# Rewriting the opening of an attention-and-MLP kernel: two blocks by halves of 256 tokens, one explicit order of operations, wider weight casts

## The chip, the cores and the metric

The kernel runs on one core of one Trainium2 chip. The metric is device time in microseconds (us). It was 305.51 us before the change (median of 3 runs, 305.02 to 306.14).

The names of the engines in the profile are PE (TensorE), PEld (TensorE's weight loads), ACT (ScalarE), DVE (VectorE), POOL (GpSimd) and SP (SyncE, which only issues DMAs here). "PEclk" is the share of TensorE's full clock that was granted. It stands at 1.00 also where the trace has no record of the clock; a slow clock there shows only in the pace of the products.

## The reference

q, k and v have the shape 8 x 8 x 576 x 64. Attention is computed within chunks of 64 tokens. Its output x has 4608 rows of 512, and it feeds an MLP with a gate that depends on the channel:

```python
# cut from the reference
scores = scale * np.matmul(q_c, k_c.transpose(0, 1, 2, 4, 3))   # chunks of 64 tokens
attn = np.exp(scores - np.max(scores, axis=-1, keepdims=True))
attn = attn / (np.sum(attn, axis=-1, keepdims=True) + 1e-09)
x = np.matmul(attn, v_c)            # then reordered to [4608, 512]
h = x @ w_in                        # 512 -> 2048
g = h * (1.0 / (1.0 + np.exp(-beta * h)))
return (g @ w_out).astype(np.float32)   # 2048 -> 512
```

Everything arrives and leaves in float32. The kernel multiplies in bfloat16, so every input is loaded and then cast.

## The kernel before

The work is cut into nine blocks of 512 tokens. For each block the kernel loads q, k and v, casts them, transposes q and k, and computes scores, exp, `attend` (the product with v), `normalize` and `turn` (the transpose of x). Then come `mm1` (the product with w_in, tanh on ScalarE, g on VectorE) and `mm2` (the product with w_out). In the first blocks all of this has to wait for data: 8 MB of weights, and 3 MB of q, k and v for each block.

A small helper class records operations per engine in program order and derives the semaphores from what each one reads and writes (`K(...)` names a piece of memory). So the order in which the Python code calls the functions is the order in which each in-order engine and DMA queue works. In this kernel that order comes from events `at(time, function, ...)`, which are sorted by their time:

```python
at(-100, make_constants)
at(-100, load_beta)

at(-99, load_qk, 0, 0)
at(-99, load_qk, 0, 1)
at(-98, load_v, 0)
for j in range(4):
    at(-97, load_w_in, j)
    at((-43, 1.5, 5.5, 9.5)[j], cast_w_in, j, ("pool",) * 4)
    at((-42.8, 1.7, 5.7, 9.7)[j], load_w_out, j)
    at((15, 20, 24, 25)[j], cast_w_out, j, ("pool",) * 4)
at(-43.5, load_qk, 1, 0)
at(-43.5, load_qk, 1, 1)
at(-42.9, load_v, 1, (0,))
at(-42.7, load_v, 1, (1,))
at(10, load_qk, 2, 0)
at(10, load_qk, 2, 1)
at(10, load_v, 2)

# ... (blocks 1 and 2)
    t0, u = base(blk - 1) + 2, 1
    loads = 24.5 if blk == 3 else t0 - 22
    for which in range(2):
        at(loads, load_qk, blk, which)
    at(loads + 0.1, load_v, blk)
    for i in range(4):
        at(35.5 if blk == 3 else t0 - 15.9, cast_qk, blk, i // 2, i % 2, "pool")
# ... (attention of the later blocks)
for blk in range(NB):
    for n in range(16):
        at(base(blk) + n, mm1, blk, n, (n + 2) % 4 if blk < 1 else n % 2)
# ...
events.sort(key=lambda e: (e[0], e[1]))
for _, _, fn, args in events:
    fn(*args)
```

The weights are loaded in quarters of 1 MB and cast by GpSimd in four instructions of 512 columns. beta is loaded near the front, on ScalarE's DMA queue:

```python
def load_beta():
    def f(e):
        with nc.allow_non_contiguous_dma(reason="beta is tiny"):
            return e.dma_start(beta_raw[:, :], beta.rearrange("(t p) -> p t", p=128))
    P.dma("act", f, writes=[K("beta_raw")])
    P.op("dve", lambda e: e.tensor_single_scalar(
        beta_half[:, :], beta_raw[:, :], 0.5, ALU.mult),
        reads=[K("beta_raw")], writes=[K("beta_half")])
# ...
def load_v(blk, us=(0, 1)):
    s, h = blk % NVS, slice(4 * us[0], 4 * us[-1] + 4)
    for b, c, m, at in chunk_pairs(blk):
        def f(e, b=b, c=c, at=at, m=m):
            r = 64 * (at % 2)
            return e.dma_start(vstage[r:r + 64 * m, s, at // 2, h, :],
                               v[b][h, 64 * c:64 * (c + m), :].rearrange("h t d -> t h d"))
        P.dma("sp", f, writes=[K("vstage", s, u, at + i, v=blk)
                               for u in us for i in range(m)])

def load_w_in(j):
    s = j % NWS

    def f(e):
        a = w_in[:, 512 * j:512 * (j + 1)].rearrange("(c p) f -> p c f", p=128)
        return e.dma_start(wstage[:, s, :].rearrange("p (c f) -> p c f", c=4), a)
    P.dma("sp", f, writes=[K("wstage", s, v=j)])

def load_w_out(j):
    s = (4 + j) % NWS

    def f(e):
        a = w_out[512 * j:512 * (j + 1), :].rearrange("(t p) d -> p t d", p=128)
        return e.dma_start(wstage[:, s, :].rearrange("p (t d) -> p t d", t=4), a)
    P.dma("sp", f, writes=[K("wstage", s, v=4 + j)])
# ... (cast_w_in likewise)
def cast_w_out(j, engines):
    s = (4 + j) % NWS
    for i, eng in enumerate(engines):
        dst = w_out_bf[:, 4 * j + i, :]
        src = wstage[:, s, 512 * i:512 * (i + 1)]
        if eng == "act":
            P.op("act", lambda e, d=dst, a=src: e.activation(d, a, AF.Copy),
                 reads=[K("wstage", s, v=4 + j)], writes=[K("w_out", 4 * j + i)])
        else:
            P.op(eng, lambda e, d=dst, a=src: e.tensor_copy(d, a),
                 reads=[K("wstage", s, v=4 + j)], writes=[K("w_out", 4 * j + i)])

```

The product with w_in always takes all 512 tokens of a block, writes one bank of the PSUM tensor F, and needs the whole x of its block:

```python
def mm1(blk, t, bank):
    sx, sg, T = blk % NXT, blk % 2, NT * blk + t
    for c in range(NC):
        P.op("pe", lambda e, c=c: e.matmul(
            F[:, bank, :], w_in_bf[:, c, 128 * t:128 * t + 128], x_of(sx, c),
            start=(c == 0), stop=(c == NC - 1)),
            reads=[K("w_in", t // 4, c), K("xT", sx, c // 2, v=blk)],
            writes=[K("F", bank, v=("h", T))])
    P.op("act", lambda e: e.activation(tt[:, T % 3, :], F[:, bank, :], AF.Tanh,
                                       scale=beta_half[:, t:t + 1]),
         reads=[K("F", bank, v=("h", T)), K("beta_half")], writes=[K("tt", T % 3, v=T)])
    P.op("dve", lambda e: e.scalar_tensor_tensor(
        g2[:, sg, t, :], tt[:, T % 3, :], 1.0, F[:, bank, :], ALU.add, ALU.mult),
        reads=[K("F", bank, v=("h", T)), K("tt", T % 3, v=T)], writes=[K("g", sg, t, v=blk)])
```

The softmax here doesn't subtract the row's maximum and nothing guards it: scores larger than these inputs give would overflow.

## Time and profile before

The median of three runs is 305.51 us. The profiled run took 303.35 us, with a span of 301.5 us and no loss of clock on record, so it is at the fast end of this kernel's runs.

The first view gives the busy time of each engine in five stretches of the profiled run of the kernel before. The columns are the stretch and its length, then the busy time and the count of instructions for PE, PEld, DVE, ACT and POOL, then PEclk, the share of the DMA engines' time, and GB/s.

```profile
...
core 0: us, PE busy (x) PEld busy (x) DVE busy (x) ACT busy (x) POOL busy (x), PEclk, DMA share, GB/s
0.00:20.00 20.00, 8.42 (x174) 6.56 (x175) 6.94 (x10) 8.62 (x11) 5.34 (x16) 1.00 1.02 269
20.00:36.00 16.00, 15.54 (x93) 7.63 (x92) 10.82 (x16) 10.78 (x16) 12.61 (x21) 1.00 1.04 325
36.00:50.00 14.00, 11.54 (x181) 5.81 (x179) 7.01 (x10) 7.65 (x12) 8.38 (x18) 1.00 1.08 349
50.00:84.00 34.00, 31.61 (x329) 15.56 (x330) 20.15 (x25) 17.97 (x27) 19.24 (x21) 1.00 1.05 271
84.00:290.00 206.00, 205.94 (x1640) 94.00 (x1639) 93.67 (x136) 103.84 (x163) 71.80 (x62) 1.00 0.64 148
...
```

TensorE does nothing else than work from 84 us on: 205.94 us of 206. A gain can only come from the first 84 us. There it idles for 11.6 us in the first 20 us, and for 0.5, 2.5 and 2.4 us in the next three stretches. DMA is full over these stretches: its share is about 1 on average in each of the first four.

The second view is the timeline of the kernel before, cut to three starts: the last cast of v for block 0, the four casts of the first w_in quarter, and the first product with w_in. Columns: start, duration, engine, source line, operation, output and input, count; in brackets the idle time just before and what ended it.

```profile
...
15.29 0.62 POOL L314 CAST v_bf<-vstage 128x512 bf16<-128x512 f32 x1 [0.52 <-DMA vstage<-in_v_dram]
...
18.01 2.29 POOL L294 CAST w_in_bf<-wstage 128x512 bf16<-128x512 f32 x4 [2.10 <-DMA wstage<-in_moe_w_in_dram]
...
20.28 1.06 PE L441 MATMUL F<-xT,w_in_bf 128*128 128x512 bf16 x2
...
```

The first product starts at 20.28 us, 2.3 us after the first quarter of w_in has landed.

The third view lists what TensorE waited for in the opening of the kernel before, from 20 to 84 us. Columns: the waiting engine and line, the releaser, total us, number of waits, the longest.

```profile
...
PE F L441 <- DVE g L449: 0.9, 2, 0.6
PE A L389 <- POOL v_bf L314: 0.8, 1, 0.8
PE F L389 <- ACT E L374: 0.8, 2, 0.6
PE A L423 <- DVE x_sb L405: 0.8, 1, 0.8
PE A L367 <- DVE qkO L314: 0.8, 1, 0.8
PE A L341 <- POOL qkcast L314: 0.4, 1, 0.4
PE F L423 <- DVE x_sb L405: 0.3, 1, 0.3
```

These waits are small, spread out, and of different kinds: v casts on GpSimd, copies and normalizing on VectorE, exp on ScalarE. They add up to 4.8 us. Measured another way, the time from the first product to the last (278.1 us) less all its products at their warm pace (269.0 us: 53.7 for the opening, 215.3 after it) is 9.1 us. That counts also the slow clock at the start (a product every 0.43 us until 22.60 us, and every 0.216 us after) and the fractions of a microsecond that a list of waits leaves out.

The fourth view is the chain of waits that ended last in the kernel before, cut to its weight loads (start, length, what):

```profile
...
31.85 6.37 DMA wstage<-in_moe_w_out_dram
38.67 11.18 DMA wstage<-in_moe_w_out_dram
49.91 1.53 POOL w_out_bf L306 x3
...
```

In this stretch the chain goes through the loads of w_out, for 17.6 us.

The page's list of the costliest groups of the kernel before gives the cost of tanh (L446) and g (L449) per product of 512 tokens. After the shapes come the count, the busy time in all and the mean ns of one, then the idle time before them and its releasers.

```profile
...
L449 DVE SCALAR_TENSOR_TENSOR g<-tt,F 128x512 bf16<-128x512 bf16 x144 | 98.9, 688 | 129.5 <-ACT tt L446 129.3
L446 ACT ACTIVATE tt<-F,beta_half 128x512 bf16<-128x512 f32 x144 | 98.9, 687 | 113.2 <-PE F L441 111.3
...
```

Both take 0.69 us against 0.863 us of TensorE for the same product. There is little room in those two engines while products of w_in follow one another.

### The profile page before, as it was taken

The numbers are of one execution on the slowest core, as the hardware profiler recorded it, in microseconds if no ns is written. First come the engines' busy times: TensorE is split into PE (matmuls) and PEld (weight loads), VectorE is DVE, ScalarE is ACT, GpSimd is POOL, SyncE is SP. The second block draws the span as 40 slices with busy tenths as digits, with TensorE's granted clock in tenths as the row PEclk, the third lists the DMA queues.
The fourth block names the chain that finished last, engine by engine and source line by source line (L and its number), as shares of the span: only waits on it lengthen the run. The fifth ranks groups of instructions, "written<-read, shape, count | busy, mean of one in ns | idle before, by whom it ended". The sixth has DMA issues, their size and how long they took to land.

```text
span 301.5 us, 5783 instructions
## 1 busy us (share of the span) xinstructions
PE 281.4 (93%) x2448; PEld 133.2 (44%) x2448; DVE 138.6 (46%) x194; ACT 150.6 (50%) x230; POOL 117.4 (39%) x134
## 2 busy tenths in 40 slices
PE   1579979988999999999999999999999999999995
PEld 1444543544444444444444444444444444444442
DVE  1447853446755543553364336433643373343300
ACT  2537754664555446544644464446444644554411
POOL 1258677742780962098085408640660000000000
PEclk9999999999999999999999999999999999999999
DMA  7999999999999579979926992798471122000121
GB/s 192 269 386 362 272 335 364 243 328 213 255 290 193 143 238 216 185 187 315 223 73 187 306 206 72 215 295 160 66 90 39 48 71 72 35 35 35 57 85 70
DMA packets 106161, 55.96 MB, mean 186 GB/s; under 512 B 79000, under 2 KB 97432, under 8 KB 106136
## 3 DMA queue, kind: packets, MB, share of 16 engines
q1 hardware_dynamic: 98944, 46.15, 63.9%
q10 hardware_dynamic: 7192, 9.45, 9.5%
q8 instruction: 19, 0.31, 0.4%
q14 instruction: 6, 0.05, 0.0%
HBM read 36.71 MB, written 9.44 MB: 153 GB/s over the span
## 4 chain that ended last, share of the span: by engine, by line
PE 80%; DMA 7%; DVE 4%; ACT 3%; SPq 1%; POOL 1%; issue 1%; ACTq 1%
PE F L456 38%; PE F L441 37%; DMA wstage<-in_moe_w_out_dram 6%; PE A L367 2%; PE A L389 2%; DMA qkstage<-in_k_dram 2%; SPq L256 1%; DVE qkO L314 1%; DVE x_sb L405 1%; ACT tt L446 1%; DVE g L449 1%; POOL w_out_bf L306 1%; ACT ostage L461 1%; ACT qkO L312 1%; ACTq L469 1%
## 5 line engine op out<-in xcount | busy, mean ns | idle before, releaser
L449 DVE SCALAR_TENSOR_TENSOR g<-tt,F 128x512 bf16<-128x512 bf16 x144 | 98.9, 688 | 129.5 <-ACT tt L446 129.3
L446 ACT ACTIVATE tt<-F,beta_half 128x512 bf16<-128x512 f32 x144 | 98.9, 687 | 113.2 <-PE F L441 111.3
L441 PE MATMUL F<-xT,w_in_bf 128*128 128x512 bf16 x576 | 147.0, 381 | 1.0 <-DVE g L449 0.9
L456 PE MATMUL F<-w_out_bf,g 128*128 128x512 bf16 x576 | 145.1, 379 | 0.0
L456 PEld LDWEIGHTS F<-w_out_bf,g 128*128 128x128 bf16 x576 | 55.5, 98 | 65.0
L441 PEld LDWEIGHTS F<-xT,w_in_bf 128*128 128x128 bf16 x576 | 54.2, 98 | 65.5 <-DVE g L449 2.4
L314 POOL COPY qkO<-qkT 128x1024 bf16<-128x1024 bf16 x22 | 42.8, 1988 | 59.2 <-DMA qkT<-qkcast 47.8
L314 POOL CAST qkcast<-qkstage 128x1024 bf16<-128x1024 f32 x32 | 32.9, 1043 | 22.8 <-DMA qkstage<-in_q_dram 11.1
L461 ACT ACTIVATE ostage<-F 128x512 f32<-128x512 f32 x36 | 21.5, 598 | 18.7 <-PE F L456 18.6
L314 POOL CAST v_bf<-vstage 128x512 bf16<-128x512 f32 (+1 forms) x40 | 23.3, 619 | 13.4 <-DMA vstage<-in_v_dram 13.4
L374 ACT ACTIVATE E<-A 128x512 bf16<-128x512 f32 x36 | 20.5, 593 | 1.3 <-PE A L367 1.3
L405 DVE TENSOR_TENSOR x_sb<-A,rec 128x1024 bf16<-128x1024 f32 x16 | 19.6, 1224 | 0.6
L341 PE MATMUL F<-identity,qkcast 128*128 128x128 bf16 x32 | 4.1, 311 | 8.6 <-DVE qkcast L314 6.9
L306 POOL CAST w_out_bf<-wstage 128x512 bf16<-128x512 f32 x16 | 9.2, 618 | 5.6 <-DMA wstage<-in_moe_w_out_dram 5.6
L294 POOL CAST w_in_bf<-wstage 128x512 bf16<-128x512 f32 x16 | 9.2, 617 | 4.3 <-DMA wstage<-in_moe_w_in_dram 3.8
L367 PEld LDWEIGHTS A<-qkO 64*64 64x64 bf16 x576 | 6.4, 113 | 8.7 <-issue 6.5
L367 PE MATMUL A<-qkO 64*64 64x64 bf16 x576 | 8.2, 200 | 2.0 <-ACT qkO L312 1.2
L389 PE MATMUL A<-v_bf,E 64*64 64x65 bf16 x512 | 8.2, 198 | 1.3 <-POOL v_bf L314 0.8
L389 PEld LDWEIGHTS A<-v_bf,E 64*64 64x64 bf16 x512 | 5.9, 109 | 7.9 <-issue 5.5
L341 PEld LDWEIGHTS F<-identity,qkcast 128*128 128x128 bf16 x32 | 3.1, 141 | 9.4 <-DVE qkcast L314 7.2
L312 ACT ACTIVATE xT<-F 128x1024 bf16<-128x1024 bf16 x3 | 3.1, 1024 | 5.4 <-PE F L423 5.4
L341 PE MATMUL A<-identity,qkcast 128*128 128x128 bf16 x64 | 4.9, 219 | 0.5 <-POOL qkcast L314 0.4
(31 smaller groups left out, 48.3 us busy)
## 6 DMA issues: line engine op xcount, KB each, us to landing
out_dram<-ostage ACTq DMA_DIRECT2D x36, 256.0 KB, 3.4
qkstage<-in_q_dram SPq DMA_DIRECT2D x32, 256.0 KB, 4.7
qkstage<-in_k_dram SPq DMA_DIRECT2D x32, 256.0 KB, 5.8
vstage<-in_v_dram SPq DMA_DIRECT2D x28, 256.0 KB, 6.5
wstage<-in_moe_w_in_dram SPq DMA_DIRECT2D x4, 1024.0 KB, 10.0
wstage<-in_moe_w_out_dram SPq DMA_DIRECT2D x4, 1024.0 KB, 8.3
vstage<-in_v_dram SPq DMA_DIRECT2D x16, 128.0 KB, 4.7
qkstage<-in_q_dram SPq DMA_DIRECT2D x8, 128.0 KB, 3.3
```

The costliest lines, as they stand in the source:

```text
L306: P.op(eng, lambda e, d=dst, a=src: e.tensor_copy(d, a), reads=[K("wstage", s, v=4 + j)], writes=[K("w_out", 4 * j + i)])
L314: P.op(eng, lambda e: e.tensor_copy(dst, src), reads, writes)
L341: P.op("pe", lambda e, n=n, i=i: e.transpose(dst[:, i, n, :], qkcast[:, which, 2 * half + n, i, :, :].rearrange("p h d -> p (h d)"), ident ...
L367: return e.matmul(A[64 * g:64 * g + 64, 2 * u + hb, col:col + 64], kT[r, 2 * cc + g, :], qT[r, 2 * cc + g, :])
L374: P.op("act", lambda e: e.activation(E[:, bank, :], A[:, bank, :], AF.Exp, scale=0.125), reads=[K("A", bank, v=("s", blk))], writes=[K("E" ...
L389: return e.matmul(ps[64 * half:64 * half + 64, bank, col:col + 65], E[r, 2 * u + hb, 256 * w + 64 * cc:256 * w + 64 * cc + 64], v_bf[r, sa ...
L405: P.op("dve", lambda e: e.tensor_tensor(x_sb[:, u, :, :, :].rearrange("p g c (h d) -> p (g c h) d", h=2).rearrange("p (b t) d -> p b t d", ...
L441: P.op("pe", lambda e, c=c: e.matmul(F[:, bank, :], w_in_bf[:, c, 128 * t:128 * t + 128], x_of(sx, c), start=(c == 0), stop=(c == NC - 1)) ...
L446: P.op("act", lambda e: e.activation(tt[:, T % 3, :], F[:, bank, :], AF.Tanh, scale=beta_half[:, t:t + 1]), reads=[K("F", bank, v=("h", T) ...
L449: P.op("dve", lambda e: e.scalar_tensor_tensor(g2[:, sg, t, :], tt[:, T % 3, :], 1.0, F[:, bank, :], ALU.add, ALU.mult), reads=[K("F", ban ...
L456: P.op("pe", lambda e, t=t: e.matmul(F[:, bank, :], g2[:, sg, t, 128 * s:128 * s + 128], w_out_bf[:, t, :], start=(t == 0), stop=(t == NT ...
L461: P.op("act", lambda e: e.activation(ostage[:, N % NOS, :], F[:, bank, :], AF.Copy, scale=0.5), reads=[K("F", bank, v=("o", N))], writes=[ ...
```

## The change

The idea is to let TensorE start on half a block. Blocks 0 and 1 are handled in halves of 256 tokens from the loads to the first product, so that half of the products can start when half of x is made. Products may use banks of both PSUM tensors, A and F. w_in comes in five pieces instead of four (the first two are half as wide), and each weight piece is cast by one GpSimd instruction. The times and formulas for everything up to time 78 are replaced by one written list of 390 operations. From block 3 or 4 on the order is the old one. "No dummy products" is part of the description of the change; neither kernel has any.

```diff
-        tt = sb("tt", [128, 3, 512], BF16)
+        NTT = 4
+        tt = sb("tt", [128, NTT, 512], BF16)
-        NOS = 3
+        NOS = 4
...
+        W_IN = ((0, 256), (256, 256), (512, 512), (1024, 512), (1536, 512))
...
+        def cast_w_in(j):
+            f0, n = W_IN[j]
+            src, keys = stage_in(j)
+            P.op("pool", lambda e: e.tensor_copy(w_in_bf[:, :, f0:f0 + n], src),
+                 reads=keys, writes=[K("w_in", t) for t in range(f0 // 128, (f0 + n) // 128)])
...
-        def mm1(blk, t, bank):
+        def mm1(blk, t, bank, ps=F, psname="F", halves=(0, 1)):
+            r = slice(256 * halves[0], 256 * halves[-1] + 256)
             for c in range(NC):
                 P.op("pe", lambda e, c=c: e.matmul(
-                    F[:, bank, :], w_in_bf[:, c, 128 * t:128 * t + 128], x_of(sx, c),
+                    ps[:, bank, r], w_in_bf[:, c, 128 * t:128 * t + 128], x_of(sx, c, halves),
...    (load_qk, load_v, scores, exp_half, attend, normalize, turn_pe: halves or pairs likewise)
-        at(-101, load_act_table)
-        at(-100, make_constants)
-        at(-100, load_beta)
-        at(-99, load_qk, 0, 0)
...    (all other events before time 78)
+        first = [
+            (load_qk, 0, 0, (1,)), (cast_qk, 0, 0, 1, "act"), (load_qk, 0, 1, (0,)),
+            (load_qk, 0, 0, (0,)), (load_qk, 0, 1, (1,)), (load_v, 0, (1,)), (load_v, 0, (3,)),
+            (load_v, 0, (0,)), (load_v, 0, (2,)), (load_w_in, 3), (cast_qk, 0, 1, 0, "act"),
+            (load_qk, 1, 1, (0,)), (load_act_table,), (make_constants,), (cast_qk, 0, 0, 0, "dve"),
...
+            (transpose_pe, 0, 1, 1, F, "F", 1, "dve"), (load_w_in, 2), (scores, 0, 0, (0,)),
+            (scores, 0, 3, (0,)), (load_beta,), (scores, 0, 2, (0,)), (exp_half, 0, 1, 0),
...    (390 operations in all)
+        events = [(-1, i, fn, args) for i, (fn, *args) in enumerate(first)] + [
+            e for e in events if e[0] >= START]
```

## The prediction

> **What bounds it now.** The timeline of TensorE and the chain of waits show four stages of the 301.5 us span.
> (1) Head: the first product starts at 20.28 us. The last k load lands at 10.51; then cast (1.06), transpose (1.05), copy (1.03), scores, exp, attend, normalize (1.23), turn and copy follow one another. The first w_in quarter lands at 18.01 only, its first cast ends at 18.6.
> (2) Opening, 20.28 to 83.09: I count 136 and 72 big products, 96 transposes and 288 small attention products. At the warm spacing in the trace (4 big products in 0.863, 8 transposes in 0.45, 32 small ones in 0.38) this is 53.7 us of 62.8, so about 9 us are lost: about 1.2 on a cold clock (0.43 per product until 22.6), the rest in eleven gaps of 0.3 to 1.0 (attend behind v casts and exp, scores behind copies, products behind VectorE). DMA is busy throughout; the last w_out quarter lands at 49.9.
> (3) 83.09 to 298.4: TensorE alone, no gap.
> (4) 3.1 us of eviction and store.
>
> **What the change can reach.** Only (1) and (2). From about block 3 the order is the old one; the fourth tt and ostage buffers buy nothing there.
>
> Head: the same 4 MB (q, k, v, then 1 MB of w_in) must land before any product, so w_in arrives at about 18.0 as before, and is now cast as one piece: from the GpSimd casts of 512 and 1024 columns (0.617, 1.043) I estimate 1.9 for 2048, ready at 19.9. The halved attention should have x for the first half at about 19.6. First product about 20.0, a gain of 0.3 only. It still starts cold: the Trainium skill, "TensorE: Matmul & The Clock Gate", Part 1, has half rate until about 3.4 us of sustained activity; before's trace agrees (0.43 falling to 0.216 at 22.6, after work that began at 18.03). I expect 1.3 lost.
>
> Opening: x of block 1 is made by halves, half of block 1's products no longer wait for all of v, w_out is loaded between the block-1 pieces, seven or eight PSUM banks (A as well as F) take products, v casts are spread. By my count of bytes (2.7 us per MB, 4.7 for v) w_out quarters are cast at about 36, 41, 46 and 50, each just ahead of its use, so DMA should not stall TensorE. Most gaps should go.
>
> Added cost: products of 256 columns cost TensorE nothing (128-column transposes already run at 0.056 each), but 64 tanh and 64 g half-pieces cost ScalarE and VectorE about 0.47 and 0.42 by estimate, against 0.69 per whole: some 8 and 5 us more. VectorE, with 1.22 copies between, is as full as TensorE in block 0; the banks hide most of it. I expect 1 to 2 us of waits there and 1 later, so 3.5 lost in place of 9.
>
> **Prediction.** Gain 0.3 + 5.5, less some slippage: about 5.5 us. Time 300.0 us, range 296.8 to 303.5; faster by over 2%: 0.38, within 2%: 0.60, slower: 0.02.
>
> **What would show it.** First product at 19.5 to 20.5, spacing cold (0.21 per 256 columns) till about 23; TensorE near gapless from 24 to 80, with waits on VectorE's g of 1 to 2 us in 20 to 38; last w_out landing at 47 to 51; the steady stage and tail unchanged; the total gained entirely before 84 us.
>
> **What would make it wrong.** Better: w_in lands earlier, or gaps vanish altogether (298 or below). Worse: VectorE or ScalarE bound on half pieces; in-order queues, where one late load or cast stalls everything behind it in the fixed order; late w_out; the clock going cold again; wide GpSimd casts slower than estimated.

## The result, and the profile after

A ratio in this document is the mean time of one kernel's fast runs over that of the other's fast runs of the same rounds, so it is not quite the ratio of the medians beside it. The brackets are 95% intervals.

| | before | after |
|---|---|---|
| median of 4 runs | 305.26 us (304.50 to 306.14) | 301.10 us (300.85 to 301.71) |
| ratio | | 0.9866 [0.9834, 0.9898] |
| profiled run, span | 303.35, 301.5 us | 301.26, 299.5 us |
| first product | 20.28 us | 21.54 us |
| last product ends | 298.35 us | 296.35 us |

The new kernel is faster by 1.3%, which is "the same" at the 2% line. Neither profiled run has a loss of clock on record after its slow start. Their spans differ by 2.0 us only, since the profiled run of before was faster than its timed runs. What follows explains these 2.0 us from the traces. A repeat on another chip gave a ratio of 0.9933 [0.9899, 0.9967] (below), which is also about 2.0 us. Why the first measurement shows twice that is not settled. It lies with the kernel before: its median was 305.26 us here and 303.87 in the repeat, that of the changed kernel 301.10 and 301.40.

The same five stretches, kernel after, with the same columns:

```profile
...
0.00:20.00 20.00, 7.71 (x169) 6.01 (x170) 6.29 (x13) 8.32 (x12) 3.66 (x12) 1.00 0.96 237
20.00:36.00 16.00, 14.73 (x137) 12.28 (x136) 12.61 (x29) 13.56 (x30) 10.27 (x8) 1.00 1.07 365
36.00:50.00 14.00, 12.73 (x207) 8.05 (x206) 10.77 (x22) 7.75 (x17) 6.04 (x6) 1.00 1.06 280
50.00:84.00 34.00, 33.56 (x370) 22.04 (x369) 22.32 (x43) 22.68 (x45) 12.85 (x13) 1.00 1.07 278
84.00:290.00 206.00, 205.95 (x1675) 94.41 (x1673) 97.32 (x140) 105.10 (x166) 71.66 (x60) 1.00 0.65 152
...
```

The steady stage is unchanged (205.95 us of 206), so the whole difference arises before 84 us. In the first 20 us TensorE does 0.71 us less than before, and in the next 16 us 0.81 us less. From 36 to 50 it does 1.19 us more, and from 50 to 84 it does 1.95 us more and idles for 0.44 us only. The change loses in the head and wins in the opening.

The head, from the timeline of the kernel after: the halving of beta on VectorE, the last GpSimd cast of v, the first cast of w_in, and the first product.

```profile
...
16.87 0.17 DVE L243 TENSOR_SCALAR beta_half<-beta_raw 128x16 f32<-128x16 f32 x1 [2.43 <-DMA beta_raw<-in_moe_beta_dram]
...
16.96 0.62 POOL L316 CAST v_bf<-vstage 128x512 bf16<-128x512 f32 x1 [1.51 <-DMA vstage<-in_v_dram]
...
19.50 1.90 POOL L295 CAST w_in_bf<-wstage 128x2048 bf16<-128x2048 f32 x1 [1.92 <-DMA wstage<-in_moe_w_in_dram]
...
21.54 0.80 PE L464 MATMUL F<-xT,w_in_bf 128*128 128x256 bf16 x3
...
```

The last cast of v starts 1.67 us later than before, at 16.96 us. The first piece of w_in is cast from 19.50 us instead of 18.01. VectorE waits 2.43 us for beta. The first product comes 1.26 us later than before, where the prediction had it 0.3 us earlier. The same 4 MB have to arrive first in both kernels, so something slowed them. The following two fences show the DMA queues from 12 to 16 us, before and then after. The first line has packets, bytes and throughput. The others have, for each queue, packets, MB, and the time their packets took as a share of 16 engines. Packets in flight overlap, so the shares may add up to more than 100%.

```profile
...
DMA packets 2088, 1.12 MB, mean 281 GB/s; under 512 B 1754, under 2 KB 1754, under 8 KB 2088
...
q1 hardware_dynamic: 2088, 1.12, 121.7%
...
```

```profile
...
DMA packets 4232, 0.67 MB, mean 166 GB/s; under 512 B 4169, under 2 KB 4169, under 8 KB 4232
...
q1 hardware_dynamic: 2168, 0.66, 94.9%
q10 hardware_dynamic: 2064, 0.01, 35.8%
...
```

In the kernel after, 2064 packets with 0.01 MB in all run on ScalarE's queue (q10). They are the load of beta: 2048 numbers of four bytes, each in a packet of its own. These packets take 35.8% of the 16 engines for 4 us, which is 11 ns of one engine for each (0.358 x 16 x 4 us / 2064), or 1.4 us of all 16, and throughput drops from 281 to 166 GB/s. In the kernel before the same load ran between 1 and 5 us, when the main queue had little to do: it carried 0.58 MB in the first 5 us. The Trainium skill, "DMA: Bandwidth & Descriptors", states that each DMA engine takes turns between the queues that have work, packet by packet (Queues, rings and completion order). The drop of the main queue, from 121.7% to 94.9%, agrees with that. So a queue of tiny packets can take a large share of the engines' time from a queue of larger ones.

What TensorE waited for in the opening of the kernel after, in the same form as before, from 21.5 to 90 us:

```profile
...
PE A L464 <- POOL w_in_bf L295: 0.9, 2, 0.6
PE F L482 <- POOL w_out_bf L305: 0.8, 1, 0.8
PE F L403 <- POOL v_bf L316: 0.5, 2, 0.3
PE A L403 <- POOL v_bf L316: 0.3, 1, 0.3
PE A L343 <- POOL qkcast L316: 0.2, 1, 0.2
```

The waits of the kernel before on VectorE and ScalarE are gone. Those that are left, 2.7 us, are on GpSimd's casts of what DMA brought. From first to last product, less 269.0 us at the warm pace, the loss is now 5.8 us (before: 9.1).

The chain of waits of the kernel after goes through w_out as before (a load and the cast behind it). In front of that, from the start to 26.58 us, it is SyncE's issuing of loads almost alone, where in the kernel before it runs through the computing engines from 10.59 to 31.85 us. Whether the issuing itself is slow, or only waits for the full DMA engines, no run tested; with beta first, issuing the four v loads took 4.92 us in place of 5.61, so it is at least in part a wait:

```profile
...
34.03 9.59 DMA wstage<-in_moe_w_out_dram
43.68 1.91 POOL w_out_bf L305
...
```

The four w_out casts start at 37.80, 43.68, 48.94 and 53.87 us (before: 38.27, 43.33, 47.13, 49.91). The list asks for them later on purpose, behind pieces of block 1.

The groups of the kernel after between 20 and 60 us, kept apart by form, give the cost of the half-size pieces of tanh (L469) and g (L473):

```profile
...
L469 ACT ACTIVATE tt<-A,beta_half 128x256 bf16<-128x256 f32 x27 | 12.4, 474 | 4.7 <-PE A L464 4.7
L473 DVE SCALAR_TENSOR_TENSOR g<-tt,A 128x256 bf16<-128x256 bf16 x27 | 11.2, 419 | 4.0 <-ACT tt L469 3.7
...
```

A half takes 0.474 and 0.419 us, so two halves cost 0.26 us more on ScalarE and 0.15 us more on VectorE than one whole (0.69). This was predicted to the second digit. No wait on g of the predicted 1 to 2 us is on the list, though; the extra banks may hide it, which was not tested.

### The profile page after: what moved, and what is told of

The parts are those of the page before. It is cut to its first block, busy times and chain, and to the rows that moved or that the text cites. A ratio compares the mean times of both kernels' runs of the same rounds, so it can differ in the third digit from the quotient of the medians.

```text
span 299.5 us, 6088 instructions
## 1 busy us (share of the span) xinstructions
PE 281.0 (94%) x2576; PEld 145.5 (49%) x2576; DVE 149.3 (50%) x244; ACT 158.7 (53%) x268; POOL 104.5 (35%) x95
## 4 chain that ended last, share of the span: by engine, by line
PE 79%; SPq 9%; DMA 8%; POOL 1%; ACT 1%; DVE 1%; issue 1%; ACTq 0%
PE F L482 39%; PE F L464 34%; SPq L260 5%; DMA wstage<-in_moe_w_out_dram 3%; DMA qkstage<-in_q_dram 2%; PE A L464 2%; DMA vstage<-in_v_dram 2%; SPq L289 2%; PE A L403 2%; SPq L271 2%; PE A L371 2%; POOL w_out_bf L305 1%; DVE qkO L316 0%; ACTq L496 0%; ACT ostage L488 0%
## 5 line engine op out<-in xcount | busy, mean ns | idle before, releaser
L473 DVE SCALAR_TENSOR_TENSOR g<-tt,F 128x512 bf16<-128x512 bf16 (+1 forms) x140 | 88.5, 634 | 108.1 <-ACT tt L469 107.8
L469 ACT ACTIVATE tt<-F,beta_half 128x512 bf16<-128x512 f32 (+1 forms) x140 | 89.9, 645 | 96.4 <-PE F L464 92.8
L464 PE MATMUL F<-xT,w_in_bf 128*128 128x512 bf16 (+1 forms) x560 | 130.3, 359 | 0.2
L488 ACT ACTIVATE ostage<-F 128x512 f32<-128x512 f32 x36 | 21.5, 598 | 19.7 <-PE F L482 19.7
L426 DVE TENSOR_TENSOR x_sb<-A,rec 128x1024 bf16<-128x1024 f32 (+1 forms) x19 | 20.6, 1084 | 0.7
L464 PE MATMUL A<-xT,w_in_bf 128*128 128x256 bf16 x144 | 19.9, 275 | 0.9 <-POOL w_in_bf L295 0.9
L469 ACT ACTIVATE tt<-A,beta_half 128x256 bf16<-128x256 f32 x36 | 16.4, 474 | 6.3 <-PE A L464 6.3
L316 POOL CAST v_bf<-vstage 128x512 bf16<-128x512 f32 x28 | 16.5, 625 | 6.5 <-DMA vstage<-in_v_dram 6.5
L473 DVE SCALAR_TENSOR_TENSOR g<-tt,A 128x256 bf16<-128x256 bf16 x36 | 14.7, 418 | 4.9 <-ACT tt L469 4.6
L464 PEld LDWEIGHTS A<-xT,w_in_bf 128*128 128x128 bf16 x144 | 13.9, 99 | 4.4 <-DVE g L473 1.5
L295 POOL CAST w_in_bf<-wstage 128x2048 bf16<-128x2048 f32 (+1 forms) x5 | 7.8, 1555 | 7.2 <-DMA wstage<-in_moe_w_in_dram 5.9
```

The source lines that it names most:

```text
L316: P.op(eng, lambda e: e.tensor_copy(dst, src), reads, writes)
L426: P.op("dve", lambda e: e.tensor_tensor(dst, o[:, :, :, 0:64], r.unsqueeze(3).to_broadcast([128, nb, 4, 64]), ALU.mult), reads=src + [K("r ...
L464: P.op("pe", lambda e, c=c: e.matmul(ps[:, bank, r], w_in_bf[:, c, 128 * t:128 * t + 128], x_of(sx, c, halves), start=(c == 0), stop=(c == ...
L469: P.op("act", lambda e: e.activation(tt[:, T % NTT, r], ps[:, bank, r], AF.Tanh, scale=beta_half[:, t:t + 1]), reads=[K(psname, bank, v=(" ...
L473: P.op("dve", lambda e: e.scalar_tensor_tensor(g2[:, sg, t, r], tt[:, T % NTT, r], 1.0, ps[:, bank, r], ALU.add, ALU.mult), reads=[K(psnam ...
L488: P.op("act", lambda e: e.activation(ostage[:, N % NOS, :], ps[:, bank, :], AF.Copy, scale=0.5), reads=[K(psname, bank, v=("o", N))], writ ...
```

## The experiments

The table gives all twelve runs, in the order of the text below. "Ratio" is to the kernel before on the same chip in the same rounds. The medians of before were 303.72 (chip 12, first four runs), 303.87 (chip 10), 304.19 (chip 8) and 304.63 us (chip 12, last run).

| run | chip | median us | ratio [95%] | first product |
|---|---|---|---|---|
| after, again | 10 | 301.40 | 0.9933 [0.9899, 0.9967] | 21.48 |
| beta first | 12 | 299.95 | 0.9877 [0.9848, 0.9907] | 21.41 |
| table first | 12 | 301.83 | 0.9940 [0.9912, 0.9967] | 21.26 |
| both first | 12 | 299.82 | 0.9872 [0.9843, 0.9900] | 20.80 |
| beta halved later | 12 | 301.33 | 0.9928 [0.9902, 0.9954] | 21.66 |
| before, beta late | 10 | 304.96 | 1.0035 [1.0010, 1.0061] | 21.57 |
| w_in in six pieces | 10 | 300.39 | 0.9870 [0.9846, 0.9895] | 19.83 |
| block 1 whole | 10 | 307.50 | 1.0130 [1.0097, 1.0163] | 21.58 |
| split casts | 8 | 299.94 | 0.9865 [0.9843, 0.9887] | 19.86 |
| half of w_out | 8 | 297.84 | 0.9788 [0.9766, 0.9810] | 20.31 |
| before, with dummy products | 8 | 304.59 | 1.0017 [0.9991, 1.0043] | 19.93 |
| cast order | 12 | 300.03 | 0.9857 [0.9833, 0.9882] | 19.80 |

### The control: the changed kernel again

The edit is none.

> The changed kernel once more, as a control on this chip and for a second profile. First product again at about 21.5 us, the first w_in cast at about 19.5, the beta load landing between 15 and 17; ratio to the kernel before between 0.983 and 0.992. The single moves of the earlier runs are then to be read against this ratio.

Measured: 301.40 us, ratio 0.9933. Its profile repeats the first one: first product at 21.48 us, w_in cast at 19.44 us, 175 GB/s between 12 and 16 us. The ratio is just outside the expected 0.983 to 0.992: one of the six runs took 304.14 us, and without it the ratio of the means would be 0.9915. The gain to explain on the later chips is thus 2.0 to 2.6 us of 304.

### Why the head is late: beta, the table, or VectorE's wait

Theory: the load of beta takes DMA time from v and w_in. Rivals: the table load holds up ScalarE; or the harm is done on VectorE, which stands still until beta has come.

Beta first, the one-line move back:

```diff
         first = [
+            (load_beta,),
             (load_qk, 0, 0, (1,)), (cast_qk, 0, 0, 1, "act"), (load_qk, 0, 1, (0,)),
...
-            (scores, 0, 3, (0,)), (load_beta,), (scores, 0, 2, (0,)), (exp_half, 0, 1, 0),
+            (scores, 0, 3, (0,)), (scores, 0, 2, (0,)), (exp_half, 0, 1, 0),
```

> One move: the beta load goes to the front of the opening (issued at about 1 us instead of 11.3). Theory A (its 2048 tiny packets take DMA engine time from v and w_in between 12 and 16 us): the stretch 12 to 16 us moves about 220 GB/s or more instead of 166, the cast of the last v piece starts at about 15.5 instead of 16.96, the first w_in cast at about 18.0 instead of 19.50, the first product at about 20.1 instead of 21.54, the time falls by 1.2 to 1.5 us against the changed kernel. Rival B (only VectorE's in-order wait for beta delays x): w_in still lands at about 19.5, the first product stays at about 21.4, the time moves by less than 0.3. Rival C (the loads are late because of the table load at 4.94 us): like B.

Table first moves `(load_act_table,)` to the front of the list in the same way, and leaves beta where it was.

> One move: the activation table is loaded at the start (at about 0.8 us) instead of at 4.94 when q has landed. Theory A: first transposes at about 6.2 instead of 7.43, the dip of DMA throughput between 4.5 and 6.5 us (about 213 GB/s) goes if the table load caused it and w_in lands up to 0.7 us earlier; otherwise the first product and the time stay within 0.3 us, since w_in and v arrive no sooner. Rival C (the table load is what made the head late): first product at about 20.3, time down by 1.2.

Both first does both moves.

> Both moves. Theory A: first product at 19.4 to 20.1, time 1.3 to 2.1 us below the changed kernel; the sum of the two single moves to within 0.4 us. If only the beta move counts, the same as that one alone.

Beta halved later leaves the load where it was and moves only VectorE's part, 0.17 us of work and a wait, behind the normalizing of block 0:

```diff
-            (cast_qk, 1, 1, 0, "dve"), (turn_pe, 0, 1, F, "F", 3, "act", (0,)),
+            (halve_beta,), (cast_qk, 1, 1, 0, "dve"), (turn_pe, 0, 1, F, "F", 3, "act", (0,)),
...    (halve_beta is the second half of load_beta, now a function of its own)
```

> The beta load stays where the change put it; only VectorE's halving of beta moves behind the four normalizations, so VectorE no longer waits for beta before the first of them. Theory A: normalizations start at about 16.0 instead of 16.96, but the last v piece still lands at about 17.0 and w_in at 19.5, so the first product stays at 21.2 to 21.6 and the time within 0.3 us. Rival B: the first product at about 20.6, the time down by 0.9 us.

These four ran on one chip in the same rounds. Beta first and both first reached 0.9877 and 0.9872; table first and beta halved later stayed at 0.9940 and 0.9928, where the control is (0.9933, on another chip). So the load of beta costs about 0.6%, or 1.8 us. VectorE's wait and the table are not what costs it. Throughput from 12 to 16 us rose from 166 to 277 GB/s with beta first.

One expectation failed all the same: the first product hardly moved (21.41 us; 21.54 in the changed kernel). The timeline of GpSimd with beta first shows why:

```profile
...
14.98 0.61 POOL L316 CAST v_bf<-vstage 128x512 bf16<-128x512 f32 x1 [0.46 <-DMA vstage<-in_v_dram]
19.37 1.89 POOL L295 CAST w_in_bf<-wstage 128x2048 bf16<-128x2048 f32 x1 [3.77 <-DMA wstage<-in_moe_w_in_dram]
...
```

The last v cast starts 2 us earlier, but w_in lands at 19.37 us, where 18.0 was expected. So where did the 1.8 us come from? From what comes after it: the whole train of loads runs earlier. Starts of the casts in the traces, in us:

| | second w_in piece | w_out 1 | w_out 2 | w_out 4 |
|---|---|---|---|---|
| beta late (after; again; table first; halved later) | 23.29; 24.00; 23.73; 23.40 | 37.80; 38.27; 37.96; 37.59 | 43.68; 43.86; 43.78; 43.03 | 53.87; 54.31; 54.63; 53.74 |
| beta first (beta first; both first; six pieces) | 22.32; 22.40; 22.54 | 36.51; 36.59; 36.86 | 41.62; 42.49; 42.23 | 52.30; 53.34; 53.07 |

With beta first the w_out casts come 1.2 to 1.5 us earlier on average, and the time falls by 1.8 us.

This profile has one more thing to teach. Its products ran at half pace for longer, as one line of each timeline shows (eight products of 256 columns; first with beta first, then the changed kernel):

```profile
...
23.92 1.91 PE L464 MATMUL F<-xT,w_in_bf 128*128 128x256 bf16 x8
...
```

```profile
...
23.50 1.04 PE L464 MATMUL F<-xT,w_in_bf 128*128 128x256 bf16 x8
...
```

With beta first the full pace came at 26.67 us, 5.26 us after the first product, in the changed kernel at 22.93 us, 1.39 us after it. By estimate that costs TensorE 2.6 and 0.7 us, yet beta first was the faster run, and no wait of 0.2 us or more on a cast is left in it after the first product. The two profiles of the changed kernel agree: half pace for 1.39 and 2.97 us, and the last product ends at 296.35 and 296.33 us. So in these traces a TensorE that is slower at the start waits less for data later. How long the slow start lasts differs between runs (1.3 to 5.3 us in the changed kernel and its variants), so the first product alone says little about the time.

### The same move in the other kernel

If the load of beta is what costs, the kernel before should suffer from it too.

```diff
-        at(-100, load_beta)
+        at(-46.6, load_beta)
```

> The kernel before, with only the beta load moved from the front to the middle of the q, k, v loads. Theory A: the stretch 12 to 16 us moves 170 to 200 GB/s instead of 281, the last v piece and the first w_in quarter come 1 to 1.7 us later, first product at 21.2 to 22.0 instead of 20.28, time 0.5 to 1.5 us above the kernel before. If the beta load were harmless: first product at 20.3, no change.

Measured: 1.0035 [1.0010, 1.0061], or 1.1 us slower, as expected. The first product moved from 20.28 to 21.57 us, the last v cast from 15.29 to 16.66, w_in from 18.01 to 19.32, and throughput from 12 to 16 us was 173 GB/s. These are the changed kernel's head times within 0.3 us. So the move of beta alone is enough to make a head as late as that. It is not the only thing that keeps the changed kernel's first product from coming earlier, since with beta first it was still at 21.41 us, where the kernel before had 20.28. That is the next question.

Its profile also shows the clock falling later on (columns as in the first view):

```profile
...
40.00:44.00 4.00, 2.17 (x68) 1.47 (x68) 2.30 (x5) 2.01 (x5) 3.48 (x8) 0.77 1.09 313
44.00:48.00 4.00, 3.78 (x21) 2.38 (x21) 1.43 (x2) 1.60 (x2) 2.29 (x4) 0.50 1.04 387
...
```

The clock fell to half at 42.19 us and came back at 49.02. TensorE had been busy for 1.95 of the last 3.41 us. How much idle time costs the clock can't be read from this: in the profile of the kernel before TensorE was busy for only 1.47 of the 3.41 us up to 42.01, and the clock stayed full.

### What holds up the first piece of w_in

In the run with beta first, 15 of the 16 completion signals of the first w_in load came within 0.48 us, and the last came 2.18 us after the first. One of the engines that share the load was held up. The line of the instruction queue in the DMA view from 17.5 to 19.5 us names a candidate:

```profile
...
q8 instruction: 1, 0.02, 3.4%
...
```

This is one 16 KB packet of the program's own instructions, which took about 1.1 us of one engine (3.4% of 16 engines for 2 us). There is one in every kernel, beginning at 17.8 to 19.2 us. The Trainium skill, "DMA: Bandwidth & Descriptors" (Why a DMA increments its semaphore by 16 and not by 1), says that a load runs on up to 16 engines that finish independently. The 16 recorded signals agree: a load is as late as its slowest engine. If the fetch delays the piece, a smaller first piece that lands before the fetch should not be delayed. So the piece of 512 columns was split into two of 256, in the kernel with both early loads:

```diff
-        W_IN = ((0, 256), (256, 256), (512, 512), (1024, 512), (1536, 512))
+        W_IN = ((0, 256), (256, 256), (512, 512), (1024, 256), (1536, 512), (1280, 256))
...    (piece 5 follows piece 3 in the loads and casts; the first products use piece 3 first)
```

> Both early moves, and the first w_in load of 512 columns cut into two of 256, the products of the first taken first. Theory D (one DMA engine loses about 1.6 us to a 16 KB instruction fetch at about 18.4 us, and any load that ends after it lands that much late): the first piece ends before the fetch, at 16.5 to 17.3, is cast by 18.3, and the first product is bound by x, at 19.2 to 20.0. Rival E (loads are merely slow, 2.7 us per MB): the first piece lands 1.35 us before the whole did, at 17.4 to 18.0, first product at 19.6 to 20.2. The time: if the opening behind it is bound by DMA (w_out), it falls by less than half of what the first product gains, 0 to 0.6 us below the kernel with both moves.

GpSimd's timeline of this run, the first two w_in casts:

```profile
...
16.66 1.04 POOL L295 CAST w_in_bf<-wstage 128x1024 bf16<-128x1024 f32 x1 [0.90 <-DMA wstage<-in_moe_w_in_dram]
18.16 1.04 POOL L295 CAST w_in_bf<-wstage 128x1024 bf16<-128x1024 f32 x1 [0.46 <-DMA wstage<-in_moe_w_in_dram]
...
```

The first half is cast at 16.66 us, 2.1 us ahead of the whole piece in the kernel with both loads early (18.77), and the first product came at 19.83. The signals of the first half spread over 0.54 us; those of the load that was in flight during the fetch spread over 1.92. This supports the fetch as the cause of the held-up signal, but a smaller piece lands earlier anyway (the rival expected it at 17.4 to 18.0 us; it landed at 16.6), and nothing was run that moves the fetch on purpose.

The traces hold better evidence, since the fetches fall at different times in them. In the last run of the table the signals of the load that began to land at 18.40 us, when the fetch began, spread over 0.42 us, and those of the next load over 1.65. In the kernel before (fetch at 18.54) it is 0.66 and 1.58. A second fetch, at 27.12 us in the former and 31.46 in the latter, puts a second engine back: the fifteenth signal comes 1.67 and 1.61 us after the first, where it was 0.40 and 0.60 before. One thing does not fit. With beta first the fetch is recorded from 18.36 to 19.45 us, and when it began, the late signal (it came at 19.32) was already 0.7 us behind the other 15. So the fetch is the likely cause, but it is not shown to be the cause.

The time says something else. The first product came 1.0 us earlier than with both loads early, yet the ratio is the same: 0.9870 against 0.9872. In the same rounds the control had 0.9933, and the difference is no more than the early beta gives by itself. An earlier first product gained nothing that could be measured.

### Are the halves of block 1 worth their cost?

Here every pair of half operations of block 1 becomes one whole operation, at the place of the second half, with attend and normalize in the banks of A. Each whole product stands where the first of its halves stood, and x is turned just before the first of them. The rest is as in the changed kernel, with beta late.

```diff
-            (scores, 1, 3, (0,)), ... (scores, 1, 3, (1,)), ... (exp_half, 1, 1, 0), ...
+            (scores, 1, 3), ... (exp, 1, 2), (exp, 1, 3), ...
-            (mm1, 1, 8, 3, F, "F", (0,)), ... (mm1, 1, 8, 2, A, "A", (1,)), ...
+            (mm1, 1, 8, 3, F, "F"), ...
```

> The changed kernel, with block 1 taken whole again (scores, exp, attend, normalize, turn and products of 512 tokens), the order otherwise kept. If the halves of block 1 are what keeps TensorE fed while v of block 1 and w_out are still on their way: TensorE waits 2 to 4 us in front of the first product of block 1, which then starts at 51 to 52 us instead of 47.85, and the time rises by 1.5 to 3 us. If the halves do nothing but add ScalarE and VectorE work: the same time or up to 1 us less.

Measured: 1.0130, 6.1 us more than the control of the same rounds, twice the highest loss that was expected (1.5 to 3 us). Two lines show the start of block 1's products, first in the changed kernel, then with block 1 whole:

```profile
...
47.85 0.60 PE L464 MATMUL F<-xT,w_in_bf 128*128 128x256 bf16 x4
...
```

```profile
...
53.66 1.89 PE L464 MATMUL F<-xT,w_in_bf 128*128 128x512 bf16 x4 [1.12 <-ACT xT L314]
...
```

They start 5.8 us later, at 53.66 us, and at half speed: four products take 1.89 us there. The window view of the same run shows the clock:

```profile
...
48.00:52.00 4.00, 2.86 (x48) 1.99 (x50) 2.09 (x4) 0.00 (x0) 1.90 (x1) 0.68 1.03 339
52.00:56.00 4.00, 2.88 (x12) 1.17 (x10) 0.42 (x1) 1.44 (x2) 1.90 (x1) 0.50 1.12 329
...
```

The clock had been cut to half before that, at 49.41 us, after TensorE had been busy for only 1.18 of the last 3.41 us. The Trainium skill, "TensorE: Matmul & The Clock Gate" (Part 1), describes two states, full and half, and a window of about 3.4 us that decides. The 0.50 here agrees with it, and so does the length of the half-clock stretch: 10.24 us, three times 3.41. The loss is thus the late start and the half clock together. The mean clock of the six runs is 0.989 (the control has 1.0), so by estimate the clock accounts for at most 1.1% of 307.5 us, or 3.5 of the 6.1 us. In the kernel before, block 1's products start at 45.27 us, earlier than in either; the changed kernel wins by having fewer gaps, not by starting block 1 earlier. This run undoes the halves within an order that was made for halves, so it shows that this order needs them, not that no order of whole blocks could do as well.

### Do the waits on casts matter?

The waits left in the six-piece kernel are on GpSimd casts of 1.9 us, where a product needs only the first part. So each cast was cut in two, and the first w_out cast was put behind the v casts:

```diff
-            P.op("pool", lambda e: e.tensor_copy(w_in_bf[:, :, f0:f0 + n], src), ...)
+            for f in range(0, n, 256):
+                P.op("pool", lambda e, f=f: e.tensor_copy(
+                    w_in_bf[:, :, f0 + f:f0 + f + 256], src[:, :, f:f + 256]), ...)
```

> The kernel of the six pieces, with the GpSimd casts of w_in and w_out quarters in two instructions of 1024 columns each, and the casts of v of block 1 ahead of the first w_out cast. In the six-piece profile TensorE waited 0.43, 0.86, 0.47 and 0.41 us for these casts and 0.38 and 0.21 for v. Each wait for a quarter should shrink by up to 0.86, the v waits by up to 0.5: together 1.5 to 2 us less waiting, time 1.0 to 2.0 us below the six pieces (ratio 0.981 to 0.984 to the kernel before) if DMA does not take it back; if the DMA supply alone sets the pace of the opening, 0.5 us or less.

Measured: 0.9865 [0.9843, 0.9887]; the six-piece kernel had 0.9870. The waits moved rather than vanished. There are 1.2 us on w_out casts, and a wait of 0.99 us that ends at 28.80 us. The list puts it down to g, which ended at 28.77; but the cast of the third w_in piece had ended at 28.66 only, and the half that is used first was cast second. (In the next run that wait is gone, so it was the cast.) A last run put these two casts in the order of use:

```diff
-            for f in range(0, n, 256):
+            for f in ((0,) if n == 256 else (256, 0) if j == 2 else (0, 256)):
...
+            ... (cast_w_out, 0, (0,)), (cast_v, 1, "pool", 0), ... (cast_w_out, 0, (2,)), ...
```

> The split casts in the order in which their halves are used: the second half of the third w_in piece first (its columns are taken first), and the two halves of the first w_out cast before and after the casts of v of block 1. In the profile of the split casts this is aimed at TensorE waits of 0.99, 0.83, 0.38 and 0.33 us. If casts set the pace: time 1 to 2 us below that run (ratio 0.980 to 0.983). If the DMA supply sets it: the wait comes back at later w_out casts and the time stays within 0.7 us (ratio 0.984 to 0.988).

Measured: 0.9857 [0.9833, 0.9882]. This is the lowest ratio of all correct kernels, but it can't be told from those of beta first (0.9877), both first, six pieces and split casts. Removing waits on casts changed the ratio by 0.1%, which is within the intervals. New waits came in their place: 0.6 us on casts of q and k, and 0.5 on g.

### Is it the amount of data?

Rival to the casts: the opening runs at the pace of DMA, and removing one wait only lets TensorE arrive earlier at the next load. In this run (its relative error is 1.585) only half of the columns of w_out are loaded: 2 MB less. Its output is wrong, which doesn't matter for the time. All instructions of the engines remain. The rest is the six-piece kernel.

```diff
-                return e.dma_start(wstage[:, j, :].rearrange("p (t d) -> p t d", t=4), a)
+                return e.dma_start(wstage[:, j, :].rearrange("p (t d) -> p t d", t=4)[:, :, 0:256],
+                                   a[:, :, 0:256])
```

> Wrong result on purpose: the kernel of the six pieces, loading only half the columns of each w_out quarter (2 MB less in the opening), everything else alike. If the opening of the changed kernel is bound by the DMA supply: w_out casts come 1.4, 2.7, 4 and 5.4 us earlier, TensorE's waits for w_out (0.47 and 0.41) go, and with them 0.5 to 1.5 us of the time. If DMA is not the bound: the same time within 0.3 us.

Measured: 0.9788 [0.9766, 0.9810] against 0.9870 [0.9846, 0.9895] for the six-piece kernel on another chip. The difference, 0.0082 of 304 us, is 2.5 us. Against split casts, in the same rounds (0.9865), it is 2.3 us. That is more than the expected 0.5 to 1.5. The number of packets did not change: 2048 of them had 1 KB in place of 2. The list of TensorE's waits from 21 to 90 us in this run is short:

```profile
...
PE A L465 <- DVE g L474: 0.8, 1, 0.8
PE F L483 <- issue: 0.3, 2, 0.2
```

No wait on a load or on a cast of a load is left. The w_out casts start at 36.00, 39.72, 44.10 and 47.14 us, the last one 5.9 us earlier than in the six-piece kernel. So this much of the loss that the six-piece kernel had left in its opening is due to the amount of data, and no rearrangement tried here recovered it.

### Is part of the gain the clock?

The runs of the kernel before aren't all at full clock. It ran 44 times: 14 runs at a mean clock of 0.998 or more took 303.41 us on average, 30 runs at 0.989 to 0.994 took 304.44. The changed kernel's ten runs are all at 0.998 or more. If the changed kernel gains partly by keeping the clock up, seven dummy products in the gap of the kernel before should gain about as much:

```diff
+        at(17.05, dummy, F, "F", 2, 3)
         at(17.1, attend, 1, 0, F, "F")
+        at(17.3, dummy, A, "A", 0, 4)
```

> The kernel before, with seven dummy products of 512 columns (1.5 us at full clock) in its two holes between 38.6 and 41 us, where it waits for exp and v of block 1. Theory F (in part of its runs the kernel before cools down in these holes and pays 1 to 2 us of half clock after them; this is why its runs spread over 3 us and why the medians differ by more than the two profiles): all runs at a granted clock of 1.0, time 0.3 to 1.2 us below the kernel before, spread below 1.5 us. Rival: the clock differs by chance, not by these holes: clocks of 0.989 to 1.0 as before, time the same or up to 0.5 us above.

Measured: 1.0017 [0.9991, 1.0043]. All six runs had a clock of 0.999 or more, against three of eleven runs of the kernel before in the same rounds. So filling the gap does keep the clock, as the theory said, but no run was faster for it (303.95 to 305.39 us). The dummies take TensorE time themselves (an estimate of 1.5 us, from seven products at 0.216), and the profile has a new wait, so the run does not exclude the clock as a part of the gain. It shows that holding the clock in this way does not pay.

The changed kernel has no such gap: between 30 and 63 us of its profile TensorE is busy for at least 2.65 us of any 3.41; in that of the kernel before this falls to 1.47. If the mean of all 44 runs of the kernel before (304.12 us) came down to that of its runs at high clock (303.41), 0.7 us would be gained; this is an estimate of the clock's share. Against it stands that two of the six runs with beta first had a clock of 0.989, and one of them was the fastest of the six (298.83 us). The clock's share of the gain stays open.

## Why the prediction was right or wrong

The time was right. The prediction was 300.0 us (296.8 to 303.5), with "same" the likeliest class; 301.10 us and 1.3% were measured. In part this is luck: the range is wide enough to hold a gain of 2 us, which is what the traces show of the promised 5.5. Two terms of its sum were mis-sized. Against the spans, which differ by 2.0 us, the promised gain is 3.5 to 3.8 us too large (5.5 us, or 0.3 + 5.5 before its allowance for slippage). The head missed by 1.6 us and the opening by 2.2.

1. **Head, "First product about 20.0, a gain of 0.3 only".** Measured 21.54, a loss of 1.26 us. The step that failed is "w_in arrives at about 18.0 as before": it counted the bytes in front of w_in, and overlooked that the load of beta had moved into that stretch. In bytes it is nothing (8 KB); in packets it is 2064. The kernel before with the same move shows the same head (21.57). Moving beta back recovers about 0.6%, seen in the train of loads and hardly in the first product: w_in was still cast from 19.37 and 18.77 us, with one of 16 signals late. So "about 18.0" failed for two reasons, beta and a delay inside the load, for which the instruction fetch is the likely cause.
2. **Opening, "3.5 lost in place of 9".** Measured 5.8 in place of 9.1. The step that failed is that w_out casts at 36, 41, 46 and 50 us are "each just ahead of its use, so DMA should not stall TensorE". They started at 37.80, 43.68, 48.94 and 53.87. About 1.3 us of the delay is beta's. The remaining waits are for what DMA delivers: with 2 MB less to load they vanished and 2.5 us with them, while earlier first products and split casts gave nothing that could be measured.
3. **Cost of the halves.** The cast of 2048 columns was estimated at 1.9 us and took 1.896. Half pieces were estimated at 0.47 and 0.42 us and took 0.474 and 0.419. The slow clock at the start was expected to lose 1.3 us; by estimate it lost 0.7 in the first profile and 1.5 in the second one of the same kernel. The "waits on VectorE's g of 1 to 2 us in 20 to 38" did not come: all that is left between 21.5 and 90 us is on casts by GpSimd.
4. **Where.** The prediction wanted to see "the steady stage and tail unchanged; the total gained entirely before 84 us", and that was right: 205.94 and 205.95 us of 206, and a tail of 3.1 us in both.
5. **Value of the halves.** The prediction put the gain into "Most gaps should go", with block 1 made by halves. The direction was right: undone in this order, they cost 6.1 us, of which at most 3.5 are the half clock's.

The best simple version is the changed kernel with the load of beta back at the front (299.95 us, 0.9877). The lowest ratio, 0.9857, belongs to the last run of the table and can't be told from it.

Still open: why the first measurement (0.9866) shows twice the gain of the repeat (0.9933), how much of either is due to the clock (0.7 us by the estimate above), and whether the instruction fetch alone holds up the load in flight.

## What to carry to other kernels

When an order is rewritten by hand, look first at the small loads that moved: a load of four-byte pieces, like the 8 KB here, belongs where DMA has nothing else to do. Here one line moved back to the front gave 0.6%, about as much as the whole rewrite had gained on the chip of the repeat (0.7%). In an opening that waits for data, count bytes and packets before waits: an earlier first product or a shorter cast only moved the wait, while less data removed it. Working in halves pays where it lets work start before its inputs are complete, but check that the extra pieces on the other engines have room, and that no gap grows long enough to cost the clock (busy for 1.18 of 3.41 us was too little here).

## What the Trainium skill lacked or had wrong

- "DMA: Bandwidth & Descriptors" gives a time per packet and the turn-taking between queues, but not what follows for others: a load of 8 KB in 2064 packets took 35.8% of 16 engines for 4 us and brought the rest down from 281 to 166 GB/s. It cost 1.1 us in one kernel and about 1.8 us in the other.
- "Runtime: NRT & Kernel Launch" (Instruction fetch mechanics) calls the cost of crossing a 16 KiB boundary "mostly hidden". That speaks of the engine that fetches. For loads in flight the traces have something else: such a packet of about 1.1 us on one DMA engine, and one of 16 signals 1.7 us after the other 15. No page has a figure for what a fetch takes from a data load. In the traces the lag comes with the fetch at its different times; no run moved the fetch on purpose.
- "TensorE: Matmul & The Clock Gate" ties the cold state in Part 1 to an idle window of about 3.4 us, and tells elsewhere (A second HAM failure mode) of frequent short idles, without saying how much idle time suffices. In the kernel before with beta late the clock fell to 0.50 at 42.19 us, after TensorE had been busy for 1.95 of the last 3.41 us, with no single pause over 0.7 us. In the kernel before, 1.47 of 3.41 us did not cost the clock. So a whole idle window is not needed, and the busy share of the last 3.41 us does not decide alone.
